# Split attention with a PReLU feed-forward layer: one mask matmul per bank ahead of the scores for batch 0's streaming heads, and a new order of the items from number 300 on

## The chip, the cores and the metric

One core of one Trainium2 chip runs the kernel. The metric is the device time of one execution in microseconds (us). Of the kernel before, three runs are known: 228.17 us in the median, 227.71 to 228.29.

## What is computed

Attention over 4 batches, 8 heads, 768 positions and 64 values per head, then a feed-forward layer on the 3072 tokens of width 512. Heads 0, 2 and 6 ("retrieval heads") are causal. The other five ("streaming heads") see only the first 4 positions (the sinks) and the last 64. The reference, cut to what matters:

```python
causal = rel >= 0
stream_keep = causal & (is_sink | in_win)          # n_sink 4, window 64
scores = where(retrieval head ? causal : stream_keep, q @ k.T / 8, -1e9)
x = softmax(scores) @ v                            # to 3072 x 512
h = x @ w_in                                       # 512 -> 2048
g = max(h, 0) + alpha * min(h, 0)
out = g @ w_out                                    # 2048 -> 512, float32
```

## The kernel before, in words

**Items and their order.** The whole kernel is a list of 1076 named items in a hand-written string, `ORDER` (L14 to L71). A loop (L807) emits them one after the other. Each engine works through its own instructions strictly in that order, and semaphores make it wait for what an instruction needs. An item's first letter says what it does:

- `L`, `C`: a load from HBM (SyncE's queue), and the cast of what was loaded to bfloat16.
- `T`/`t` (batches 0 and 1): queries or keys are transposed on TensorE and copied out. `D` (batches 2 and 3): they are transposed by a DMA from SyncE's queue (`dma_q` L321, `dma_k` L336).
- `S`, `s`, `m`: scores of a part of one head on TensorE, exp of them on ScalarE, and, from segment 4 on, the multiplication with a 0/1 mask on VectorE.
- `A`, `a`: the product with v (L553), then division by the row sum on VectorE (`AV_out`, L563 and L564).
- `X`: the head pair's result is turned into the feed-forward layer's input xT, by a DMA transpose from SyncE's queue (`X_dma`, L568) for segments 4 to 14.
- `P`, `p`, `g`: first feed-forward product (`P1`, L598), ScalarE's part of PReLU (L603), VectorE's part (L610).
- `O`, `o`: second product in quarters (`P2`, L618), copy out on ScalarE (L624) and the store, from GpSimd's queue (L628).

**Tiling.** Work comes in 16 segments, n = 0 to 15: four per batch, each a pair of heads from `PAIRS` = (2,6), (1,5), (0,4), (3,7). So `S12.0.3` is the fourth part of the scores of the first head of segment 12, the first segment of batch 3. The feed-forward layer works in 8 blocks of tokens, two per batch (512 and 256 tokens), so `P4.8` belongs to the first block of batch 2. A `P` item adds up four matmuls over the four segments of its batch, in the order of the segments. So the first `P2` item needs X4, X5, X6 and X7 one after the other, the first `P4` item X8 to X11, and the first `P6` item X12 first.

**What fixes the order around the change.** `P`, `O` and attention items of different batches are mixed in `ORDER`, so that TensorE has matmuls of the feed-forward layer to do while ScalarE and VectorE work on attention. PSUM has 8 banks of 128 x 512 float32. Which bank an item gets is settled when the kernel is built, by the order (`take`, `give`). SyncE's queue issues loads and DMA transposes in the order of the items, one after the other.

**Bursts.** Scores of segments from 4 on aren't emitted at once: `one_score` (L412) collects them, and `emit_burst` (L418) writes them out when an item comes that can't stand beside them (`beside_burst`, L435). If both heads of a pair of row halves have at least 576 columns, the matmuls use only 64 rows each, and those of the two heads run side by side on the two halves of the array (L431). Otherwise they run one after the other (L424).

**The masks of batch 0.** Segments 0 to 3 are masked by adding -30000 in PSUM: for streaming heads, each score matmul of 192, 148 or 44 columns (L414, started by `start=True`) is followed by a matmul of the identity with a mask of the same width (L502), which adds to it. `THIRD` (L482) lists the widths: seven per head, and two or three fill one bank with 384 columns. The masks `nms` and, for the last width, `nms6` are made on GpSimd (`sink_mask`, L267). Segments 1 and 3 have two streaming heads each, and segment 2 has one: five heads with 35 mask matmuls.

Of the kernel before, what the change touches and what calls it, by code (L numbers as in the profile page):

```python
# [31 lines left out]
s6.1.0 O0.3.1 a5.1 s4.0.5 O0.3.2 O0.3.3 m4.0.1 m4.0.5 Cv4 tq7 S7.0.0 S6.0.5 S7.1.1 S4.1.1 Lk9 Lk10 Lq9 o0.2 o0.3
S4.1.3 S7.0.1 A5.0 s4.1.1 s7.0.0 m4.0.0 a5.0 X5 A4.0 s7.0.1 Lk11 s7.1.1 a4.0 s4.1.3 O1.1.0 m4.1.3 Cv7 s6.0.5 m7.0.0
m7.1.1 Lq8 S7.1.0 S6.0.4 S7.0.2 S4.1.5 S6.0.1 S7.1.2 S6.1.1 O1.1.1 Cv6 s7.1.0 O1.0.0 s4.1.5 m7.0.1 s6.1.1 m4.1.5
m6.1.1 s7.1.2 m6.1.0 s7.0.2 m7.0.2 S6.0.2 S4.1.2 S6.1.2 S6.0.0 s6.0.4 s4.1.2 s6.0.1 s6.1.2 O1.0.1 m6.0.5 m7.1.0 m4.1.1
m4.1.4 m7.1.2 m6.1.2 S6.0.3 A4.1 s6.0.0 m6.0.0 m6.0.1 A7.1 O1.1.2 A6.1 s6.0.3 m6.0.4 m6.0.3 s6.0.2 a4.1 a6.1 A6.0 A7.0
a6.0 O1.1.3 O0.0.0 O0.0.1 O0.0.2 O1.0.2 m10.0.2 O1.0.3 O0.0.3 o0.0 X4 X6 a7.1 a7.0 X7 P2.9 P2.3 p2.9 P3.4 Ck9 Cq9 g2.9
P2.14 p2.14 g2.14 Cq8 p3.4 Lq10 Lq11 Dk8.0 P2.10 p2.10 Dk9.1 o1.0 p2.3 g2.3 g3.4 Dk8.1 P3.2 P3.14 P3.12 P2.8 Dq8 P2.1
P3.8 o1.1 p3.2 Dk9.0 Lv10 g2.10 Dq9 p3.14 P2.7 Ck10 g3.2 p3.12 g3.12 g3.14 P2.2 p2.2 g2.2 Cq10 Dq10 P2.11 p2.1 g2.1
p2.11 p2.8 g2.11 P3.6 P2.5 p2.5 g2.5 P2.13 p2.13 g2.8 g2.13 P2.0 p2.0 g2.0 p2.7 P3.0 p3.0 P2.4 S8.0.5 Lv8 Lv11 P2.15  # L40
P2.12 s8.0.5 Cq11 g3.0 p2.15 g2.7 g2.15 S8.0.0 p2.12 g2.12 Ck11 p3.6 S9.0.2 P2.6 p2.6 g3.6 s8.0.0 p2.4 g2.4 g2.6
s9.0.2 p3.8 P3.10 g3.8 p3.10 O3.0.0 O2.0.0 S8.1.5 s8.1.5 O3.0.1 O2.0.1 g3.10 m8.0.0 Cv8 S8.1.3 S9.0.0 S8.0.3 S9.1.1
S8.0.1 S9.1.0 s8.1.3 s9.1.0 s8.0.1 s9.0.0 s8.0.3 m8.0.3 m8.0.1 O2.0.2 O2.0.3 o2.0 Dk10.1 Lv9 m9.0.0 Cv9 m8.0.5 Dk11.0
m9.1.0 m9.0.2 S8.0.4 S9.0.1 S10.1.1 S8.1.4 Dq11 s8.1.4 Lq13 Lk13 O3.0.2 Dk10.0 s9.1.1 s10.1.1 s9.0.1 s8.0.4 O3.0.3
o3.0 Dk11.1 S10.1.0 S10.1.2 m9.0.1 S11.0.2 S9.1.2 S8.0.2 S11.0.0 s9.1.2 Cv10 m9.1.1 A9.0 s11.0.2 s10.1.0 O2.3.0 m9.1.2
A9.1 a9.0 a9.1 X9 s10.1.2 s11.0.0 O2.3.1 Lq15 Lv14 Lq12 S8.1.0 S11.0.1 S10.0.3 m10.1.0 s8.0.2 S10.0.1 S8.1.2 S8.1.1
S10.0.0 O2.3.2 s8.1.2 s8.1.0 m8.1.4 Cq13 s11.0.1 s8.1.1 m11.0.2 m10.1.2 m8.0.4 m11.0.0 A8.0 s10.0.0 m8.1.5 m10.1.1
O2.3.3 a8.0 S11.1.2 S10.0.4 S11.1.0 S10.0.5 S10.0.2 m8.1.3 m11.0.1 s10.0.3 s10.0.1 S11.1.1 s11.1.2 A10.1 s11.1.1
O2.2.0 O2.1.0 s10.0.4 m6.0.2 m10.0.1 Cv11 m8.1.1 m8.1.0 a10.1 m10.0.4 Ck13 m10.0.0 m11.1.2 A11.0 A8.1 O2.1.1 s10.0.2
s10.0.5 o2.3 s11.1.0 Dk13.0 m11.1.1 m10.0.3 m10.0.5 m11.1.0 A10.0 a11.0 a8.1 a10.0 O3.1.0 A11.1 Cq12 O2.2.1 O2.2.2  # L50
O2.2.3 a11.1 X8 O2.1.2 O3.1.1 O3.1.2 X10 o2.2 O3.1.3 O2.1.3 X11 P4.11 o2.1 P4.14 P5.14 p5.14 P4.4 P4.6 Lk12 P5.0 g5.14
Ck12 p4.4 p4.6 p4.11 P4.13 g4.6 p4.14 g4.11 Lq14 g4.14 P5.12 P4.5 P4.12 p4.13 Dq12 o3.1 p5.0 g4.13 Cq14 g5.0 Dk13.1
p4.5 g4.5 g4.4 Cv14 P4.9 p4.9 g4.9 P4.2 P5.2 Dq13 p5.12 g5.12 P4.10 p5.2 P4.8 P4.1 p4.12 g4.12 g5.2 p4.10 g4.10 Lv15
Dk12.0 Dk12.1 Lv12 p4.1 Lk14 Lv13 Lk15 g4.1 P4.7 P4.0 p4.2 g4.2 p4.8 g4.8 p4.0 p4.7 g4.7 P4.15 Cv12 S13.0.1 s13.0.1
S12.0.5 S12.0.3 P4.3 P5.4 g4.0 s12.0.3 p4.3 s12.0.5 S12.1.5 S12.0.1 S12.0.0 S13.1.1 s13.1.1 Dq14 g4.3 Cq15 Ck14
m12.0.3 O4.3.0 s12.1.5 s12.0.1 O4.3.1 O4.3.2 s12.0.0 p4.15 g4.15 P5.6 P5.10 S12.1.1 S12.0.4 S12.0.2 p5.4 S13.1.0 g5.4
p5.6 s12.0.4 Dk14.0 P5.8 s13.1.0 s12.0.2 p5.8 s12.1.1 m12.0.0 g5.6 O4.3.3 Ck15 p5.10 g5.8 m12.0.1 g5.10 m12.0.4 O5.1.0
Cv13 O5.1.1 O5.1.2 o4.3 Dk14.1 S14.1.1 S14.0.0 S12.1.4 S14.0.1 S14.1.0 S13.0.2 m12.1.1 s14.1.0 s13.0.2 O4.2.0 m12.0.5
A12.0 s14.0.1 s12.1.4 O5.1.3 Dk15.1 s14.1.1 Dk15.0 s14.0.0 a12.0 m14.0.1 Dq15 o5.1 O4.2.1 S13.1.2 S12.1.2 S14.1.2
S14.0.4 m13.1.0 m14.0.0 m13.0.1 S14.0.5 S13.0.0 O4.2.2 O4.2.3 s13.1.2 m13.1.2 m13.1.1 s13.0.0 s14.0.4 s14.0.5 m13.0.2  # L60
S12.1.0 m12.1.5 s14.1.2 S12.1.3 S15.0.0 S14.0.3 m13.0.0 A13.1 o4.2 s12.1.0 s12.1.2 A13.0 s15.0.0 O5.0.0 s12.1.3
s14.0.3 m14.0.4 Cv15 a13.1 O5.0.1 a13.0 S15.0.1 S15.0.2 m12.1.0 S15.1.0 S15.1.2 S15.1.1 S14.0.2 O4.1.0 s15.0.2 s15.1.0
m12.1.4 s14.0.2 s15.1.1 m14.1.1 m14.0.5 m14.1.2 m12.1.3 m14.1.0 A12.1 m14.0.3 A14.1 A14.0 a14.0 s15.1.2 a14.1 m15.0.2
s15.0.1 a12.1 O4.1.1 X13 O4.0.0 O4.0.1 O4.0.2 O4.0.3 m15.0.0 m15.1.1 O4.1.2 m15.0.1 m15.1.2 m15.1.0 A15.0 o4.0 A15.1
a15.0 O4.1.3 a15.1 O5.0.2 X15 O5.0.3 X14 x15 o4.1 o5.0 X12 P6.11 p6.11 P6.2 P6.15 P6.10 p6.10 P7.4 P6.0 P6.1 g6.11
g6.10 p6.1 P6.6 P7.8 p6.15 g6.15 g6.1 p6.0 g6.0 P6.5 p7.4 p6.5 p6.6 g7.4 g6.6 g6.5 P6.3 P6.12 P7.2 p6.3 p6.12 g6.12
# [8 lines left out]
def kernel(  # L75
# [336 lines left out]
    def one_score(n, hh, m, to, keys, queries, stop=True):  # L412
        if n < 4:
            nc.tensor.matmul(to, keys, queries, start=True, stop=stop)  # L414
# [69 lines left out]
    def thirds(n, m):  # L484
        return (range(0, 2), range(2, 3))[m] if n < 4 else range(m, m + 1)

    def S_stream(n, hh, m):
# [8 lines left out]
        for x, part in enumerate(thirds(n, m)):
            o = 0
            for j, w in THIRD[part]:
                one_score(n, hh, m, sc[:, x, o:o + w], kt[:, 128 * j:128 * (j + 1)],
                          qt[:, 124 * j:124 * j + w], n >= 4)  # L500
                if n < 4:
                    nc.tensor.matmul(sc[:, x, o:o + w], ident, (nms6 if j == 6 else nms)[:, 0:w],  # L502
                                     start=False, stop=True)
# [344 lines left out]
```

## Time and profile before

| what | value |
|---|---|
| median of 3 runs | 228.17 us (227.71 to 228.29) |
| the profiled execution's own time | 228.43 us |
| its span in the profile | 225.8 us, so 2.6 us lie around it |
| TensorE (PE) busy | 221.6 us, 2005 matmuls |
| VectorE (DVE), ScalarE (ACT), GpSimd (POOL) busy | 149.1, 140.1, 45.9 us |
| granted TensorE clock | 1.00 from 5.7 us on |
| moved by DMA | 37.39 MB, mean 166 GB/s |

How to read it: the span runs from the first to the last instruction of one profiled execution. Times in the text that stand alone ("at 80.72") are microseconds from the span's start. A matmul's own duration overlaps with the next one's, so its cost to TensorE is the distance from one start to the next. A DMA has an issue (an instruction in the issuing engine's queue) and a landing (the last of its semaphore events in the trace).

### The profile page before, as it was taken

Reading aid. Unit: us, or ns where it says so; the run is one execution under the profiler, and the core shown is the slowest. Engines: PE = TensorE matmul, PEld = TensorE weight load, DVE = VectorE, ACT = ScalarE, POOL = GpSimd, SP = SyncE. Lnnn points to the kernel's source line nnn. Section 1 sums busy time; section 2 is a strip of 40 time slices with the busy share of each in tenths; the row PEclk is TensorE's granted clock in tenths of the full one; section 3 lists DMA queues with packets and bytes.
Section 4 is the critical chain, followed back from the end, with each engine's and each line's share of the span. In section 5 each row is a group of like instructions: output and inputs, shape, how many; then the busy total and the mean of one; then the engine's idle time right before and its main releaser. Section 6 shows DMA issues by size and latency. Waiting matters only on the chain.

```text
span 225.8 us, 5241 instructions
## 1 busy us (share of the span) xinstructions
PE 221.6 (98%) x2005; PEld 136.5 (60%) x2005; DVE 149.1 (66%) x393; ACT 140.1 (62%) x286; POOL 45.9 (20%) x91
## 2 busy tenths in 40 slices
...
PEclk9999999999999999999999999999999999999999
DMA  6999999999999999999989999976924420000213
GB/s 201 311 240 214 281 223 285 197 196 231 204 284 182 117 232 231 170 167 190 268 160 177 226 243 129 238 156 117 119 94 38 120 93 0 0 3 1 93 68 119
DMA packets 95417, 37.39 MB, mean 166 GB/s; under 512 B 82440, under 2 KB 93600, under 8 KB 95392
## 3 DMA queue, kind: packets, MB, share of 16 engines
...
q8 instruction: 15, 0.25, 0.5%
...
## 4 chain that ended last, share of the span: by engine, by line
PE 98%; DVE 0%; issue 0%; DVEq 0%
PE P L598 37%; PE P L618 36%; PE P L553 7%; PE P L431 4%; PE P L414 3%; PE P L688 3%; PE P L364 2%; PE P L637 2%; PE P L424 1%; PE P L502 1%; PE P L578 1%; PE P L463 0%; PE P L362 0%; DVE kT L387 0%; DVE ot L646 0%
## 5 line engine op out<-in xcount | busy, mean ns | idle before, releaser
L610 DVE SCALAR_TENSOR_TENSOR g<-neg,oma,P 128x256 bf16<-128x256 f32 (+1 forms) x128 | 70.9, 608 | 36.9 <-ACT neg L603 36.4
L598 PE MATMUL P<-xT,w_in_b 128*128 128x512 bf16 (+1 forms) x512 | 86.6, 326 | 0.0
L618 PE MATMUL P<-w_out_b,g 128*128 128x512 bf16 x368 | 85.3, 379 | 0.0
L603 ACT ACTIVATE neg<-P 128x512 f32<-128x512 f32 x96 | 54.2, 600 | 26.3 <-PE P L598 20.9
L598 PEld LDWEIGHTS <-w_in_b 128*128 128x128 bf16 x512 | 49.5, 98 | 32.3 <-DVE g L610 0.2
L618 PEld LDWEIGHTS <-g 128*128 128x128 bf16 x368 | 33.9, 98 | 37.2 <-issue 1.0
L470 ACT ACTIVATE eR<-P 128x448 bf16<-128x448 f32 (+4 forms) x63 | 36.9, 635 | 5.8 <-PE P L431 2.5
L624 ACT COPY ot<-P 128x512 f32<-128x512 f32 x23 | 13.9, 605 | 37.1 <-PE P L618 32.3
L628 POOL DMA_DIRECT2D out_dram<-ot x18 | 10.3, 572 | 111.0 <-ACT ot L624 110.8
L518 ACT ACTIVATE eS<-P 128x352 bf16<-128x352 f32 x45 | 20.8, 489 | 3.4 <-PE P L431 3.0
L564 DVE TENSOR_TENSOR xn<-P,rcp 128x448 bf16<-128x448 f32 (+1 forms) x32 | 19.5, 608 | 1.1
L529 DVE TENSOR_TENSOR eS<-eS,ms_near 128x352 bf16<-128x352 bf16 x45 | 14.9, 346 | 0.6 <-ACT eS L518 0.5
L563 DVE RECIPROCAL rcp<-P 128x7 f32<-128x7 f32 (+1 forms) x32 | 6.3, 198 | 10.9 <-PE P L553 10.8
L480 DVE TENSOR_TENSOR eR<-eR,mr_near 128x128 bf16<-128x128 bf16 (+5 forms) x54 | 10.7, 227 | 4.3 <-ACT eR L470 4.1
L414 PE MATMUL P<-qT,kT 128*128 128x192 bf16 (+14 forms) x68 | 11.2, 251 | 0.2 <-DVE kT L387 0.2
L553 PEld LDWEIGHTS <-eS 128*128 128x128 bf16 x260 | 9.5, 97 | 2.3 <-issue 0.6
L553 PE MATMUL P<-vb,eS 128*128 128x65 bf16 x260 | 10.7, 193 | 0.0
L431 PE MATMUL P<-qT,kT 64*128 64x176 bf16 (+10 forms) x168 | 10.5, 252 | 0.0
L431 PEld LDWEIGHTS <-kT 64*128 64x128 bf16 x168 | 6.7, 94 | 6.2 <-issue 5.5
L553 PE MATMUL P<-vb,eR 128*128 128x65 bf16 x276 | 10.5, 193 | 0.0
L553 PEld LDWEIGHTS <-eR 128*128 128x128 bf16 x276 | 9.5, 97 | 1.3
L646 DVE COPY ot<-P 128x128 f32<-128x128 f32 x1 | 0.3, 291 | 14.3 <-PE P L637 14.3
...
## 6 DMA issues: line engine op xcount, KB each, us to landing
...
```

What stands on the lines that cost most here:

```text
L414: nc.tensor.matmul(to, keys, queries, start=True, stop=stop)
L431: nc.tensor.matmul(to, keys[own], queries[own], start=True, stop=True)
L470: nc.scalar.activation(ebuf[n, hh][:, lo:hi].rearrange("p (x c) -> p x c", x=len(parts)), P[:, got[0]:got[0] + len(parts), 0:(hi - lo) // ...
L518: nc.scalar.activation(slots, sc[:, 0:352].rearrange("p (s c) -> p s c", c=176), AF.Exp, scale=scale)
L529: nc.vector.tensor_tensor(slots, slots, ms_near[:, 0:2, :] if m == 0 else ms_near[:, 1:3, :], op=ALU.mult)
L553: nc.tensor.matmul(pav[:, i, :], e[:, o:o + 128], vv[:, j, hh, 0:D + 1], start=(m == 0), stop=(m == len(terms) - 1))
L564: nc.vector.tensor_tensor(xn[n][:, 0:nt, D * hh:D * hh + D], pav[:, :, 0:D], rcp.to_broadcast([128, nt, D]), op=ALU.mult)
L598: nc.tensor.matmul(psg[:, w * i:w * (i + 1)], w_in_b[:, c, 128 * fb:128 * (fb + 1)], xT[:, c, o:o + w], start=(x == 0), stop=(x == 3))
L603: nc.scalar.activation(neg[t, f], bank(held["P", t, f][0]), AF.Relu, scale=-1.0)
L610: nc.vector.scalar_tensor_tensor(g_buf[t % 2][:, fb, 0:w], neg[t, f][:, c], oma[:, fb:fb + 1], bank(got[0])[:, c], op0=ALU.mult, op1=ALU.add)
L618: nc.tensor.matmul(bank(held["O", t, s][0]), g_buf[t % 2][:, f, 128 * s:128 * (s + 1)], w_out_b[:, f, :], start=(f == 0), stop=(f == 15))
L624: nc.scalar.copy(ot, bank(got[0]))
```

## The change

There are two parts.

**Masks.** For each bank of a streaming head in batch 0, one matmul of the identity with a mask of 384 columns comes first and starts the bank. The scores of this bank then add to it, with no mask behind each. The last third (192, 148 and 44 columns) has a mask of its own, the second row of a new tile `nms2`. GpSimd makes it with one copy more.

```diff
-    nms = const.tile([128, 192], bf16, name="nms")
-    nms6 = const.tile([128, 44], bf16, name="nms6")
+    nms2 = const.tile([128, 2, 192], bf16, name="nms")
+    nms = nms2[:, 0, :]
...
-        nc.gpsimd.tensor_copy(nms6, nms[:, 0:44])
-        nc.gpsimd.memset(nms6[0:NSINK, 0:NSINK], OUT)
+        nc.gpsimd.tensor_copy(nms2[:, 1, 0:148], nms[:, 0:148])
+        nc.gpsimd.tensor_copy(nms2[:, 1, 148:192], nms[:, 0:44])
+        nc.gpsimd.memset(nms2[0:NSINK, 1, 148:148 + NSINK], OUT)
...
         for x, part in enumerate(thirds(n, m)):
+            nc.tensor.matmul(sc[:, x, 0:384].rearrange("p (a c) -> p a c", c=192), ident,
+                             nms2 if part == 2 else nms2[:, 0:1, :].to_broadcast([128, 2, 192]),
+                             start=True, stop=False)
+        for x, part in enumerate(thirds(n, m)):
             o = 0
             for j, w in THIRD[part]:
-                one_score(n, hh, m, sc[:, x, o:o + w], kt[:, 128 * j:128 * (j + 1)],
-                          qt[:, 124 * j:124 * j + w], n >= 4)
-                if n < 4:
-                    nc.tensor.matmul(sc[:, x, o:o + w], ident, (nms6 if j == 6 else nms)[:, 0:w],
-                                     start=False, stop=True)
+                nc.tensor.matmul(sc[:, x, o:o + w], kt[:, 128 * j:128 * (j + 1)], qt[:, 124 * j:124 * j + w],
+                                 start=False, stop=o + w == 384)
                 o += w
```

**Order.** The same 1076 items are kept. Items 0 to 299 stay where they are; from number 300 (about 48 us into the span) to number 1019 they stand in a new order. SyncE's queue keeps its order: all its 154 loads, transposes and stores are issued in the same sequence. What moves are the matmuls, the exps, the casts and the copies around them. Three stretches, first before and then after. The end of batch 1's attention:

```
before: ... A6.1 s6.0.3 m6.0.4 m6.0.3 s6.0.2 a4.1 a6.1 A6.0 A7.0 a6.0 O1.1.3 O0.0.0 O0.0.1 O0.0.2 O1.0.2 m10.0.2 O1.0.3
        O0.0.3 o0.0 X4 X6 a7.1 a7.0 X7 P2.9 P2.3 p2.9 P3.4 Ck9 Cq9 ...
after:  ... A7.0 m6.0.0 m6.1.1 A6.1 m6.0.3 a7.1 Ck9 m6.0.5 a4.1 a6.1 s6.0.2 X4 A6.0 a6.0 X6 Ck8 a7.0 X7 Lq10 O0.0.1 Cq8
        O1.0.1 O0.0.2 O0.0.3 o0.0 O1.0.2 O1.0.3 P2.14 ...
```

The end of batch 2's attention and the way to batch 3's first scores:

```
before: A10.0 a11.0 a8.1 a10.0 O3.1.0 A11.1 Cq12 O2.2.1 O2.2.2 O2.2.3 a11.1 X8 O2.1.2 O3.1.1 O3.1.2 X10 o2.2 O3.1.3 O2.1.3
        X11 P4.11 o2.1 ... 18 more P items, o3.1 and SyncE's items as below ... S13.0.1 s13.0.1 S12.0.5 S12.0.3
after:  A10.0 a8.1 O2.2.2 O2.2.3 o2.2 m11.1.2 Lv14 Lq12 Dk13.0 a10.0 A11.1 a10.1 O2.1.0 O2.1.1 X8 a11.1 X10 X11 Lk12
        O2.1.2 O2.1.3 P4.8 P4.6 P4.11 P4.14 P4.10 P5.2 P4.5 P4.1 Lq14 Dq12 Dk13.1 Dq13 P5.12 Lv15 P4.4 P5.14 O3.1.3
        Dk12.0 Dk12.1 Lv12 P5.6 o2.1 o3.1 P4.13 P4.0 S12.0.3     (p, g and C items between them are left out)
```

The end of batch 3's attention:

```
before: A12.1 m14.0.3 A14.1 A14.0 a14.0 s15.1.2 a14.1 m15.0.2 s15.0.1 a12.1 O4.1.1 X13 O4.0.0 O4.0.1 O4.0.2 O4.0.3 ...
        A15.0 o4.0 A15.1 a15.0 O4.1.3 a15.1 O5.0.2 X15 O5.0.3 X14 x15 o4.1 o5.0 X12 P6.11
after:  A12.1 O5.0.3 a14.0 O4.0.2 a14.1 O4.1.2 X14 a12.1 O4.1.3 a15.0 a15.1 X15 O4.0.3 x15 X12 P6.4
```

More of the change, by code (lines that the diff above doesn't have):

```diff
@@ L32 @@
[L32 to L66, printed above, removed]
@@ new lines @@
+s4.0.4 m4.0.4 s6.1.0 O0.2.3 o0.2 A5.1 O0.3.2 O0.3.3 a5.1 Cv4 o0.3 S4.1.1 S7.0.1 S4.1.3 S6.0.5 S7.1.1 S7.0.0 s4.1.3
+s7.1.1 m4.1.4 ro1 m4.0.0 A5.0 a5.0 A4.0 s4.1.1 O1.1.0 s6.0.5 S6.0.4 S7.1.0 S6.1.1 a4.0 m4.1.0 s7.0.0 S7.0.2 S6.0.1
+s7.0.1 m7.0.1 S4.1.5 s7.1.0 m7.1.0 s6.0.4 m6.1.0 Lq9 X5 O1.1.1 O1.1.2 S6.0.3 S6.0.2 s6.0.1 m6.0.1 S4.1.2 Lk11 s4.1.5
+S7.1.2 m6.0.4 m4.1.5 S6.1.2 m4.1.1 s6.1.1 S6.0.0 m4.1.3 Lq8 O1.1.3 near1 s7.0.2 O0.0.0 s7.1.2 Cv6 m7.1.1 m7.1.2 A7.1
+s6.1.2 m6.1.2 m10.0.2 s6.0.3 m7.0.0 s6.0.0 O1.0.0 s4.1.2 A4.1 m7.0.2 A7.0 m6.0.0 m6.1.1 A6.1 m6.0.3 a7.1 Ck9 m6.0.5
@@ new lines @@
+a4.1 a6.1 s6.0.2 X4 A6.0 a6.0 X6 Ck8 a7.0 X7 Lq10 O0.0.1 Cq8 O1.0.1 O0.0.2 O0.0.3 o0.0 O1.0.2 O1.0.3 P2.14 P3.12 P2.9
+p2.9 P2.6 p2.14 Lq11 g2.14 g2.9 p3.12 g3.12 P2.7 P2.10 p2.10 g2.10 P2.1 p2.1 g2.1 Dk8.0 P2.2 Dk9.1 Dk8.1 Cq9 p2.2 g2.2
+p2.7 g2.7 p2.6 P2.3 P2.13 p2.13 g2.6 Ck10 Dq8 Cq10 P2.5 P2.11 Dk9.0 p2.5 P2.4 o1.0 o1.1 g2.5 g2.13 p2.11 g2.11 S8.0.0
+s8.0.0 Lv10 Ck11 P3.4 Dq9 Dq10 Lv8 p2.4 g2.4 Lv11 P2.8 p2.8 P3.2 Cq11 p2.3 p3.2 g3.2 g2.3 P3.0 g2.8 p3.0 g3.0 P2.0
+p2.0 g2.0 S8.1.5 s8.1.5 P3.6 P3.14 p3.14 g3.14 P2.15 p3.6 g3.6 p2.15 g2.15 S9.0.2 s9.0.2 S8.0.5 P2.12 P3.10 P3.8 p3.4
@@ new lines @@
+g3.4 p3.8 Dk10.1 Lv9 O3.0.0 O3.0.1 p2.12 g2.12 O2.0.0 O2.0.1 p3.10 s8.0.5 S9.0.0 g3.8 S8.0.1 S8.0.3 S9.1.1 g3.10
+m6.0.2 S8.1.3 S9.1.0 s9.1.1 m9.1.1 s9.1.0 s8.1.3 O2.0.2 O2.0.3 s8.0.3 S10.1.1 S9.0.1 s9.0.0 S8.1.4 s8.0.1 S8.0.4
+s8.0.4 m9.1.0 m8.1.5 Cv10 s9.0.1 s10.1.1 m9.0.2 m8.0.1 Dk11.0 Cv8 Dq11 O3.0.2 m8.0.0 O3.0.3 S11.0.2 S11.0.0 s8.1.4
+S8.0.2 S10.1.2 S9.1.2 o2.0 Lq13 Lk13 S10.1.0 Cv9 O2.3.0 m9.0.0 s9.1.2 s10.1.0 m9.0.1 m8.0.4 m10.1.1 m9.1.2 Dk10.0
+Dk11.1 o3.0 A9.0 s11.0.0 A9.1 m8.1.4 m8.0.5 O2.3.1 m8.0.3 s8.0.2 A8.0 a9.0 a9.1 s10.1.2 S8.1.1 s11.0.2 S10.0.3 S11.0.1
@@ new lines @@
+m11.0.2 S8.1.2 S8.1.0 S10.0.0 s10.0.0 m10.0.0 s8.1.0 a8.0 O2.3.2 O2.3.3 m8.1.0 O3.1.0 s11.0.1 s8.1.1 S10.0.4 m8.1.1
+m11.0.1 S11.1.0 s10.0.3 o2.3 S11.1.2 S11.1.1 s8.1.2 S10.0.5 S10.0.1 O3.1.1 s10.0.5 Cq13 Cv11 s11.1.1 S10.0.2 m11.0.0
+s10.0.4 s10.0.1 A11.0 O3.1.2 m8.1.3 A8.1 m10.0.4 m10.1.0 s10.0.2 a11.0 s11.1.0 m10.1.2 m11.1.0 A10.1 m10.0.3 O2.2.0
+O2.2.1 Ck13 s11.1.2 m10.0.1 X9 Lq15 m10.0.5 m11.1.1 A10.0 a8.1 O2.2.2 O2.2.3 o2.2 m11.1.2 Lv14 Lq12 Dk13.0 a10.0 A11.1
+a10.1 O2.1.0 O2.1.1 X8 a11.1 X10 X11 Lk12 O2.1.2 O2.1.3 P4.8 p4.8 Cq12 P4.6 p4.6 g4.8 P4.11 P4.14 P4.10 p4.10 P5.2
@@ new lines @@
+p4.14 g4.6 g4.14 Ck12 P4.5 p4.5 g4.5 P4.1 Lq14 Dq12 Dk13.1 p4.1 g4.10 Dq13 P5.12 Lv15 P4.4 Cv14 p5.2 g5.2 p4.4 g4.4
+P5.14 O3.1.3 p5.12 g4.1 Dk12.0 Dk12.1 Lv12 P5.6 g5.12 p4.11 Cq14 p5.14 g4.11 o2.1 p5.6 o3.1 g5.6 g5.14 P4.13 p4.13
+g4.13 P4.0 p4.0 S12.0.3 s12.0.3 S13.0.1 P4.12 p4.12 g4.12 s13.0.1 Lk14 Lv13 P4.2 p4.2 P5.0 g4.0 p5.0 g4.2 g5.0 m12.0.3
+S12.0.5 s12.0.5 Cv12 P4.3 p4.3 S13.1.1 Lk15 S12.0.0 S12.1.5 S12.0.1 s12.0.1 m12.0.1 s12.1.5 P5.4 p5.4 g4.3 s13.1.1
+m13.1.1 P4.9 p4.9 s12.0.0 P4.7 Ck14 p4.7 g5.4 P5.8 p5.8 g4.7 g5.8 Cq15 Dq14 Dk14.0 Dk14.1 P5.10 m12.1.5 P4.15 S12.1.1
```

20 lines of the change are left out of this document (15 added, 5 removed).

## The prediction, made before the changed kernel ran

> **What bounds the kernel now.** I read the page first. TensorE (PE) is busy for 98% of the span, at full clock, and the chain that ended last is PE for 98%:
>
> ```profile
> PE 221.6 (98%) x2005; PEld 136.5 (60%) x2005; DVE 149.1 (66%) x393; ACT 140.1 (62%) x286; POOL 45.9 (20%) x91
> ...
> PEclk9999999999999999999999999999999999999999
> DMA  6999999999999999999989999976924420000213
> ...
> PE 98%; DVE 0%; issue 0%; DVEq 0%
> ```
>
> The reader should see two things: an engine without gaps, and DMA engines that are nearly as full until about 165 us. But "busy" hides waits, because a matmul's row lasts longer than its distance to the next. So I read the timeline of PE for distances between starts:
>
> ```profile
> 20.54 0.24 PE L414 MATMUL P<-qT,kT 128*128 128x192 bf16 x1
> 20.62 0.24 PE L502 MATMUL P<-nms,ident 128*128 128x192 bf16 x1
> 20.70 0.25 PE L414 MATMUL P<-qT,kT 128*128 128x192 bf16 x1
> ...
> 21.49 0.18 PE L414 MATMUL P<-qT,kT 128*128 128x44 bf16 x1
> 21.52 0.18 PE L502 MATMUL P<-nms,ident 128*128 128x44 bf16 x1
> ```
>
> Each 192-column matmul costs 0.082 us (a row of 0.24 us), a 44-column one 0.028. In the same way 512 columns cost 0.216, 384 cost 0.163, 256 cost 0.109, and 65 cost 0.029. Starts further apart than these distances are rare: 0.78 us of waits before 26 us, 0.14 at 52.9, and around each of the 15 split bursts (L431) about 0.10 ahead and 0.13 within and behind. Else nothing. So the time is PE's sum of distances, plus each wait that a new order creates; no later slack pays a wait back. That is why I weigh the change by waits.
>
> **Masks.** Removed: 25 x 0.082 + 5 x 0.064 + 5 x 0.028 = 2.51 us. Added: 15 of 384 columns x 0.163 = 2.45 us (no row shows a mask of this form; rows of 384 columns elsewhere range from 0.161 to 0.164, so 2.42 to 2.46). Gain 0.06. All of it falls before 26 us, where PE also waits for VectorE's and ScalarE's copies, so part becomes waiting: 0 to 0.06. GpSimd's extra copy (0.22 us by the 44-column row) falls into its idle 0.85 us ahead of the cast at 4.69: nothing.
>
> **Bursts.** Walking through both orders with L435's rule gives 15 split bursts in each. Taking for each the larger half of its matmuls' distances, the sum goes from 7.99 to 7.93 us; the unsplit ones go from 3.03 to 3.05. Gain 0.04. Together PE's sum falls by 0.1 us.
>
> **The waits that the order creates.** SyncE's sequence is unchanged, so what matters is which producer now comes later and which consumer earlier. In before, the nearest escape was the first P2 item: X7 landed at 80.29 and its matmul ran at 80.72. X11 had 2.9 us to spare, X12 3.0, Dk12.0 (needed by S12.0.3) 4.7. I laid the same places out in the new order.
>
> First P2 item. VectorE's rows (timeline, 73 to 77 us):
>
> ```profile
> 73.84 0.21 DVE L563 RECIPROCAL rcp<-P 128x7 f32<-128x7 f32 x1
> 74.08 0.62 DVE L564 TENSOR_TENSOR xn<-P,rcp 128x448 bf16<-128x448 f32 x1
> 74.62 0.20 DVE L563 RECIPROCAL rcp<-P 128x7 f32<-128x7 f32 x1
> 74.85 0.63 DVE L564 TENSOR_TENSOR xn<-P,rcp 128x448 bf16<-128x448 f32 x1
> 75.39 0.20 DVE L563 RECIPROCAL rcp<-P 128x7 f32<-128x7 f32 x1
> 75.62 0.62 DVE L564 TENSOR_TENSOR xn<-P,rcp 128x448 bf16<-128x448 f32 x1
> 76.16 0.62 DVE L334 CAST natk<-kf 128x896 bf16<-128x896 f32 x1
> ```
>
> They are a6.0, a7.1, a7.0, then Ck9. In the new order a7.1 (0.78) and Ck9 (0.53) stand ahead of a6.0, and Ck9 and Ck8 (1.06) ahead of a7.0. So a6.0 ends at 74.70 + 1.3 = 76.0 and a7.0 at 76.24 + 1.1 = 77.3; the masks moved about may add 0.2. X7 can't issue before 77.35 and, at the landing time of 2.80 that X7 had, lands at 80.15 to 80.35; its matmul is at 80.72 - 0.1 = 80.6. No wait, by 0.3. But X6's issue took 2.66 us in before (the queue's instruction held up), against 1.25 for most transposes. If X6 again holds the queue that long from 76.05, X7 issues at 78.8, lands at 81.6, and PE waits 1.0. Bounds 0 to 1.2; I take 0.2, near the common row.
>
> First P4 item and S12.0.3. X10 waits for a10.1, and a10.1 now stands behind a10.0 on VectorE. From the start of A10.0's last matmul: 0.19 us to its end, 0.03 to a10.0, 1.70 for a10.0 and a10.1 (rows at 122.45 and 123.69: 0.86 to the end of each, 0.84 from one to the next), 0.03 to the issue: X10 issues 1.95 us after. X11 follows 1.34 later and lands 2.81 after that: 6.1. PE until the first P4 item's fourth matmul: A11.1 0.38, six O items of four matmuls 5.18, three matmuls 0.65: 6.2. So X11 is just in time (bounds 0 to 0.3; I take 0).
>
> Then the SyncE queue, from X8, X10, X11 at 122.56 on:
>
> ```profile
> 122.56 3.92 SPq L572 DMA_TRANSPOSE xT<-xn  x3
> 126.54 1.16 SPq L246 DMA_DIRECT2D kf<-in_k_dram  x2
> 127.74 1.39 SPq L212 DMA_DIRECT2D qf<-in_q_dram  x2
> 129.23 1.75 SPq L322 DMA_TRANSPOSE qT<-natq  x1
> 131.03 1.30 SPq L338 DMA_TRANSPOSE kT<-natk  x1
> 132.38 2.03 SPq L322 DMA_TRANSPOSE qT<-natq  x1
> ...
> 136.92 3.70 SPq L338 DMA_TRANSPOSE kT<-natk  x2
> ```
>
> There is no gap: each issue follows the one ahead, and none waits for a producer. So Dk12.0 comes a fixed stretch after X10: issued at 136.92 - 123.90 = 13.0 after, landed (142.19) 18.3 after. In the new order S12.0.3 is the consumer, with this PE work between A10.0's last matmul and it: A11.1 0.38, six O items 5.18, fourteen P items and O3.1.3, 15 x 0.865 = 12.98: 18.5 us. Dk12.0 lands 1.95 + 18.3 = 20.2 after the same point. **PE waits 1.7 us.** What stands behind S12.0.3 on PE is everything, and nothing can pass. The lower bound is 0: with transposes at 1.3, loads at the shortest distances in that stretch (11.4 us) and the shortest landing of a transpose in the trace (2.75), Dk12.0 lands 16.1 after A10.0's point.
>
> What could shorten it? The DMA view for 124 to 142 us:
>
> ```profile
> q1 hardware_dynamic: 11026, 2.73, 89.1%
> q0 software_dynamic: 305, 0.99, 16.4%
> ```
>
> Engines are full, and the stores (q0) take 16.4%, three of them in 18 us. In the new order o2.1 and o3.1 stand behind P5.6, just ahead of S12.0.3, so two of the three leave this stretch: 2/3 x 16.4% x 18 = 1.97 us of work, as much as the wait. If the engines' load sets the pace, Dk12.0 is in time. But the same chain reaches Dk14.1, 31.4 us after X10 (123.90 to 155.33), needed by the burst that begins at S14.1.0. By the sum of PE's distances that burst starts 32.5 us after A10.0's point, Dk14.1 lands at 33.4: 0.9 us late, and by then both stores are back. So 0 to 1.7 in all for these two places (they are one delay, not two); I take 0.9.
>
> The Trainium skill ("DMA: Bandwidth & Descriptors", "Queues, rings and completion order") states that each DMA engine goes round between the queues for which it has work, packet by packet. By that rule the stores that leave would speed up SyncE's transfers at once and the sum would be about 0.9 us less; the trace shows both queues served at a time, but not by what rule.
>
> First P6 item. X12 is issued about 1.0 us after A12.1's end if VectorE is free, lands 2.8 later; PE has four O items, X15's transposes and O5.0.3 ahead, 4.7 us: 0.8 to spare. No wait.
>
> Elsewhere, banks and exps: the nearest row is the 0.14 at 52.9 (a wait for a copy of keys), which can go or come again. Bounds -0.14 to +0.3; I take 0.1.
>
> **Sum**, in the profiled execution: 225.8 - 0.1 + 0.2 + 0.9 + 0.1 = 226.9 us of span, plus the 2.6 around it, 229.5 against its 228.43. That execution is 0.26 above the median of 228.17, so I forecast 228.17 + 1.1 = **229.3 us**.
>
> **Rivals.**
>
> *Everything lands in time* (not slower). The mechanism is the stores that leave the stretch, with X6 no longer held because X4 finds the loads ahead of it already landed. For it: X8, X10 and X11 issue at 1.34 us each. It decides if X10 to Dk12.0 takes less than 16.6 us and X10 to Dk14.1 less than 30.6 instead of 18.3 and 31.4. Then only PE's sum counts: 228.17 - 0.1 = 228.1. Chance 0.28.
>
> *Both delays in full.* X6 holds the queue (1.0 to 1.2) and the chain stays as measured (1.7), with 0.1 to 0.3 elsewhere: +2.8, 231.0. Against it: part of the first delay also moves what follows. Chance 0.20.
>
> *Faster.* Masks that need no keys run while PE would wait, so the exps of the streaming heads start earlier and the 0.78 us of waits before 26 us go: 228.17 - 0.1 - 0.78 = 227.3. Against it: the longest (0.33 at 12.3) ends with a copy of keys on VectorE, which is busy without a gap from 9.0 to 13.2, and no streaming head's scores start late in the trace. Chance 0.07.
>
> That the masks don't do what they say would move nothing: they are worth 0.06.
>
> **How the numbers follow.** Forecast 0.45 (+0.7 to +2.0), rivals 0.28, 0.20 and 0.07. The range reaches from the in-time case to the full delays: 228.0 to 231.0. About 0.3% (0.7 us) is what a measurement can tell from no change. Slower by more than that: nearly all of the forecast and the second rival, 0.64; within: 0.29; faster: 0.07.
>
> **What would show it.** In the changed kernel, PE should have gaps in starts ahead of S12.0.3's scores (L425) at about 142 us, or ahead of the burst at about 156 us, and perhaps in the first P2 item (L600, third or fourth matmul) at 80 to 82 us, each ended by a DMA's landing. 15 masks at 0.163 apart would confirm the first part. If PE has no such gaps and the time is near 228.1, the chain from X10 was shorter than measured before. A time under 227.5 would say that the early waits were PE's to remove.

## The result and the profile after

The changed kernel takes **230.26 us** in the median of six runs (229.55 to 230.90), against 227.94 us for the kernel before, measured in turn with it on the same chip. The ratio is 1.0102, with a 95% interval of 1.0079 to 1.0125: slower by 2.3 us, where 1.1 was forecast. In all ratios of this text, executions that took over 1.5% longer than the fastest of their kernel are left out (one or two in six of the kernels, among them two of 591 us), while the medians are over all executions.

The profiled execution has a span of 228.9 us and took 230.58 us itself. These lines of its page answer to those shown of before:

```profile
PE 220.3 (96%) x1958; PEld 134.8 (59%) x1985; DVE 149.4 (65%) x393; ACT 140.5 (61%) x286; POOL 46.2 (20%) x92
...
PEclk9999999999999999999999999999999999999999
DMA  6999999999998899999979799984913321000213
...
PE 64%; DMA 10%; issue 7%; DVE 7%; SPq 6%; ACT 4%; POOL 1%; DVEq 0%; POOLq 0%; ACTq 0%
```

TensorE has 1985 matmuls now (the weight loads are complete, 27 records of matmuls are missing). The clock is full throughout. What changed is the last line: the chain that ended last was TensorE for 98%, and now leaves it for DMAs, VectorE and queues. TensorE waits. The view of TensorE's waits says for what (us in total, times, longest):

```profile
PE P L600 <- DVE g L612: 1.2, 2, 1.0
...
PE P L600 <- DMA xT<-xn: 1.2, 2, 0.8
```

L600 is the first feed-forward product (L598 in before; the lines behind the edit are one or two higher). The idle time in this view begins where the last matmul ended, so it is smaller than what the time loses. The loss is the distance between starts, less the 0.216 us of a 512-column matmul (0.109 for 256 columns, 0.029 for 65). The timeline of TensorE shows the places (start, duration, then in brackets the idle time and what ended it):

```profile
64.57 0.79 PE L555 MATMUL P<-vb,eR 128*128 128x65 bf16 x21
...
81.04 2.33 PE L600 MATMUL P<-xT,w_in_b 128*128 128x512 bf16 x14 [0.36 <-DMA xT<-xn]
...
98.34 1.91 PE L600 MATMUL P<-xT,w_in_b 128*128 128x256 bf16 x12 [0.95 <-DVE g L612]
...
101.09 1.13 PE L600 MATMUL P<-xT,w_in_b 128*128 128x512 bf16 x5 [0.29 <-DVE g L612]
...
133.15 2.10 PE L600 MATMUL P<-xT,w_in_b 128*128 128x512 bf16 x9 [0.83 <-DMA xT<-xn]
```

By distances between starts, TensorE lost 0.28 us ahead of 64.57 (A4.0), 0.52 ahead of 81.04 (P2.14's fourth matmul, for X7), 1.12 ahead of 98.34 (P3.6), 0.16 at 100.2 and 0.45 ahead of 101.09 (both for banks), and 0.99 ahead of 133.15 (P4.8's fourth matmul, for X11). That is 3.52 us; before had one such wait behind 26 us, of 0.14. At S12.0.3 (145.5 us) and at the burst of S14.1.0 (159.4 us), where the prediction put the main wait, there is none.

### The profile page after: what moved, and what is told of

It is laid out like the page before. It is cut to its first block, busy times and chain, and to the rows that moved or that the text cites. A ratio compares the mean times of both kernels' runs of the same rounds, so it can differ in the third digit from the quotient of the medians.

```text
span 228.9 us, 5178 instructions
## 1 busy us (share of the span) xinstructions
PE 220.3 (96%) x1958; PEld 134.8 (59%) x1985; DVE 149.4 (65%) x393; ACT 140.5 (61%) x286; POOL 46.2 (20%) x92
## 4 chain that ended last, share of the span: by engine, by line
PE 64%; DMA 10%; issue 7%; DVE 7%; SPq 6%; ACT 4%; POOL 1%; DVEq 0%; POOLq 0%; ACTq 0%
PE P L620 23%; PE P L600 23%; PE P L555 6%; SPq L242 4%; DMA xT<-xn 3%; PE P L432 3%; DMA vf<-in_v_dram 3%; DMA qT<-natq 2%; DMA qf<-in_q_dram 2%; DVE g L612 2%; PE P L639 2%; PE P L365 1%; ACT eR L471 1%; PE P L415 1%; ACT neg L605 1%
## 5 line engine op out<-in xcount | busy, mean ns | idle before, releaser
L600 PE MATMUL P<-xT,w_in_b 128*128 128x256 bf16 (+1 forms) x501 | 86.4, 325 | 3.0 <-DVE g L612 1.2
L620 PE MATMUL P<-w_out_b,g 128*128 128x512 bf16 x352 | 83.6, 379 | 0.9 <-issue 0.2
L605 ACT ACTIVATE neg<-P 128x512 f32<-128x512 f32 x96 | 55.0, 601 | 32.5 <-PE P L600 23.4
L600 PEld LDWEIGHTS <-w_in_b 128*128 128x128 bf16 x512 | 49.4, 98 | 34.6 <-issue 2.3
L630 POOL DMA_DIRECT2D out_dram<-ot x18 | 9.8, 547 | 119.6 <-ACT ot L626 119.6
L690 PE MATMUL P<-busy 128*128 128x128 bf16 x73 | 6.7, 259 | 1.2 <-DVE busy L289 1.2
```

What stands on the lines that cost most here:

```text
L600: nc.tensor.matmul(psg[:, w * i:w * (i + 1)], w_in_b[:, c, 128 * fb:128 * (fb + 1)], xT[:, c, o:o + w], start=(x == 0), stop=(x == 3))
L605: nc.scalar.activation(neg[t, f], bank(held["P", t, f][0]), AF.Relu, scale=-1.0)
L620: nc.tensor.matmul(bank(held["O", t, s][0]), g_buf[t % 2][:, f, 128 * s:128 * (s + 1)], w_out_b[:, f, :], start=(f == 0), stop=(f == 15))
```

## The experiments

Twelve kernels ran, each in turn with the kernel before on the same chip. The chips differ (e1 to e4 on one, e5 to e8, e9 to e11 and e12 on others), so kernels are compared by their ratios. The theory, after the result: masks and bursts do nothing, and each wait above has one late producer behind it. The rival: the stretches are full, and a wait that is taken away comes back at the next item.

| run | kernel | median, us | ratio to before (95%) |
|---|---|---|---|
| e1 | new masks, before's order | 227.96 | 0.9994 (0.9981 to 1.0006) |
| e2 | old masks, new order | 230.60 | 1.0102 (1.0079 to 1.0124) |
| | after | 230.26 | 1.0102 (1.0079 to 1.0125) |
| e3 | after, Cq11 later | 229.19 | 1.0043 (1.0025 to 1.0060) |
| e4 | after, stores o1.0 and o1.1 earlier | 229.42 | 1.0078 (1.0052 to 1.0104) |
| e5 | after, Ck9 and Ck8 behind X7 | 230.16 | 1.0089 (1.0059 to 1.0119) |
| e6 | after, O3.1.3 ahead of P4.8 | 230.69 | 1.0125 (1.0089 to 1.0162) |
| e7 | after, Cv4 ahead of o0.2 | 229.68 | 1.0061 (1.0029 to 1.0092) |
| e8 | e3, e5, e6 and e7 together | 229.81 | 1.0095 (1.0060 to 1.0129) |
| e9 | e6, two stores back in X10's stretch | 231.52 | 1.0132 (1.0072 to 1.0192) |
| e10 | e5, O1.0.0 behind X7 | 230.26 | 1.0071 (1.0034 to 1.0107) |
| e11 | e8, O1.0.0 behind X7, Cq14 later | 228.71 | 1.0017 (0.9990 to 1.0043) |
| e12 | e11, s4.1.2 earlier, Cv14 later | 229.25 | 1.0055 (1.0029 to 1.0081) |

The edits are moves of items in `ORDER`; the diffs show only the items around them.

### Which part costs: e1 and e2

e1 has the new masks and before's order; e2 the old masks and the new order.

> The new masks with the order of before. Theory 'late transfers' (the whole slowdown comes from the new order: TensorE waits for X7 in the first P2 item, 0.5 us, for a PSUM bank while VectorE stands in Cq11 behind Dq9, 1.7 us, and for X11 in the first P4 item, 1.0 us): no change that can be measured, 0 to -0.2 us against before, masks 0.163 us apart. Rival 'masks' (a mask that starts a whole bank ahead of the scores costs time, in itself or by making exps wait longer): +0.5 us or more.

> The new order with the masks of before. 'Late transfers': as slow as the changed kernel, +2.2 to +2.5 us against before, with the same three waits on TensorE (0.5 at 80, 1.7 between 97 and 101, 1.0 at 132). 'Masks': nearer to before, +1.5 us or less.

e1 is level with before and e2 with after, both within 0.25%. **The order costs everything, the masks nothing.** (e1 has times, but no profile that can be compared.) In e2's profile the waits are shared out otherwise than in after's: 1.49 us at P2.14's fourth matmul, 0.46 at P4.8's, none at 97 us. So they are no fixed sum: the same order gives other waits in another execution.

### The wait at 97 us: e3 and e4

VectorE's timeline in after, at that place:

```profile
93.89 0.74 DVE L612 SCALAR_TENSOR_TENSOR g<-neg,oma,P 128x512 bf16<-128x512 f32 x1
96.94 0.56 DVE L316 CAST natq<-qf 128x768 bf16<-128x768 f32 x1 [2.31 <-issue]
```

The cast is Cq11. VectorE stands still for 2.31 us in front of it, and the g items behind it, which free TensorE's banks, stand still with it. The page names no releaser ("issue"), but the code does: `NATQ` has two buffers (L181), so Cq11 overwrites the queries that the DMA transpose Dq9 reads. Dq9 was issued at 91.38 and landed at 96.86; Cq11 starts 0.08 us later. In before Dq9 landed 3.23 us after its issue, not 5.48, and Cq11 stood 2.8 us behind that. The stores o1.0 and o1.1 are issued at 91.46 and 91.99 in after; in before they were at 86.1 and 87.1, ahead of Dq9. Cq11 in before, without a wait:

```profile
97.46 0.55 DVE L315 CAST natq<-qf 128x768 bf16<-128x768 f32 x1
```

```diff
-P2.8 p2.8 P3.2 Cq11 p2.3 p3.2 g3.2 g2.3 P3.0 g2.8 p3.0 g3.0 P2.0 p2.0 g2.0 S8.1.5
+P2.8 p2.8 P3.2 p2.3 p3.2 g3.2 g2.3 P3.0 g2.8 p3.0 g3.0 P2.0 p2.0 g2.0 Cq11 S8.1.5
```

> The changed kernel with one item moved: Cq11 stands behind g2.0, some 4 us of TensorE work later. 'Late transfers': VectorE no longer idles 2.3 us behind Dq9, the waits between 97 and 101 go, -1.0 to -1.7 us against the changed kernel (+0.6 to +1.3 against before); the waits for X7 and X11 stay. Rival 'banks' (TensorE at 97 waits because of the order of the P items and their banks, whatever VectorE does): no change, +2.3 against before.

e3 is 0.6% faster than after, as expected. Its Dq9 was as late (5.32 us), but Cq11 now comes behind the g items and waits for nothing, and TensorE has no wait between 95 and 102 us:

```profile
99.91 0.55 DVE L316 CAST natq<-qf 128x768 bf16<-128x768 f32 x1
```

e4 leaves Cq11 where it is and issues the two stores at 88.1 us, some 3 us earlier:

```diff
-P2.1 p2.1 g2.1 Dk8.0 P2.2 ... Dk9.0 p2.5 P2.4 o1.0 o1.1 g2.5
+P2.1 p2.1 g2.1 o1.0 o1.1 Dk8.0 P2.2 ... Dk9.0 p2.5 P2.4 g2.5
```

> The changed kernel with the stores o1.0 and o1.1 moved ahead, from behind P2.4 (issued at 91.2 and 91.7) to behind g2.1 (about 85 us). If Dq9's landing (5.5 us after its issue, in before 3.2) is late because these two stores share the DMA engines with it: Dq9 lands 1.5 to 2.5 us earlier, VectorE's idle time in front of Cq11 shrinks from 2.3 to under 0.8, and the time falls by 0.8 to 1.7 us against the changed kernel. If the stores have no part in it (the loads Lv10 ahead of Dq9 in its own queue hold it): no change, +2.3 against before.

By the ratios it gained about 0.5 us, less than expected, and the intervals overlap. Dq9 landed after 3.23 us, as the theory said, but Cq11 still had to wait for it, for 0.51 us:

```profile
95.58 0.56 DVE L316 CAST natq<-qf 128x768 bf16<-128x768 f32 x1 [0.51 <-DVE g L612]
```

It starts 0.08 us behind Dq9's landing (95.50) again, and TensorE still loses 0.29 at 100 us. So the place of Cq11 is shown as the cause of the loss. What makes Dq9 late goes with the time of the stores, and not with their place in `ORDER`. GpSimd's timelines in after and in e5, where Dq9 is issued at 91.38 and 92.67:

```profile
91.46 1.07 POOL L630 DMA_DIRECT2D out_dram<-ot  x2 [11.70 <-ACT ot L626]
...
93.38 1.08 POOL L630 DMA_DIRECT2D out_dram<-ot  x2 [12.61 <-ACT ot L626]
```

| first of the two stores | profiles | Dq9 lands after, us |
|---|---|---|
| 0.04 to 0.19 us behind Dq9's issue | after, e3, e6, e7, e8, e9, e11 | 5.2 to 6.1 |
| 0.63 to 0.87 us behind it | e2, e5, e12 | 3.1 to 3.6 |
| over 4 us ahead of it | before, e4 | 3.2 |

Only e4 moved the stores by intent, so this is a pattern of twelve profiles; what happens in the DMA engines no run shows.

### GpSimd's queue: e7

The 0.28 us at A4.0 came in each of the profiles with Cv4 in its new place. GpSimd's timeline in after:

```profile
63.02 0.56 POOL L630 DMA_DIRECT2D out_dram<-ot  x1 [2.28 <-ACT ot L626]
63.57 0.94 POOL L350 CAST vb<-vf 128x896 bf16<-128x896 f32 x1
```

The cast is Cv4, which makes A4.0's values. Its load had landed at 62.50, but it stands behind o0.2's store, and that waits for ScalarE's copy. The cast ends at 64.51, A4.0 starts at 64.57. In before Cv4 stood ahead of o0.2 and started at 62.76, when its load had landed:

```profile
62.76 0.93 POOL L349 CAST vb<-vf 128x896 bf16<-128x896 f32 x1 [1.55 <-DMA vf<-in_v_dram]
```

```diff
-O0.2.3 o0.2 A5.1 O0.3.2 O0.3.3 a5.1 Cv4 o0.3
+O0.2.3 Cv4 o0.2 A5.1 O0.3.2 O0.3.3 a5.1 o0.3
```

> The kernel after with the cast of values Cv4 moved ahead of the store of o0.2 on GpSimd, where the kernel before has it. Theory (a queue that the order moved it behind): in after the cast starts at 63.57, behind the issue of a store that waits for its eviction, and ends at 64.51, when A4.0 starts 0.28 us late; ahead of the store it starts when its load has landed (62.5) and ends about 63.4, the wait of 0.28 us at A4.0 is gone, and the time falls by 0.1 to 0.3 us, to 229.9 to 230.1. Rival: the 0.28 us is the price of the change of weights or is taken up by the waits behind it: 230.2, and the gap ahead of A4.0 stays.

The gap at A4.0 is gone, here and in e8, e11 and e12. (e7's profiled execution took 234.89 us, for a wait at 29 us that the last section shows; e8's shows the same without it.) The time fell by 0.9 us against after by the ratios, with intervals that just overlap; 0.28 of it is explained by this gap.

### The transfers X7 and X11: e5, e6 and e10

> The kernel after with two casts of keys (Ck9, Ck8) moved behind X7 on VectorE. Theory (late transfers): the casts stand ahead of a6.0 and a7.0, so both end about 0.6 us earlier, X7 is issued and lands about 0.6 us earlier, and the wait at the fourth matmul of P2.14 (0.52 us in the profile of after, 1.49 with the order alone) shrinks by about 0.6 us; the other waits stay, and they may take up some of it: 0.2 to 0.7 us less than after, about 229.6 to 230.1. Rival: X7 is held by the queue behind X6's own issue, not by a7.0, and the wait and the time stay as they are.

```diff
-a7.1 Ck9 m6.0.5 a4.1 a6.1 s6.0.2 X4 A6.0 a6.0 X6 Ck8 a7.0 X7 Lq10
+a7.1 m6.0.5 a4.1 a6.1 s6.0.2 X4 A6.0 a6.0 X6 a7.0 X7 Ck9 Ck8 Lq10
```

The rival was right: the time is after's, and the wait in this profile is larger, 1.43 us. SyncE's and TensorE's timelines:

```profile
75.12 5.89 SPq L574 DMA_TRANSPOSE xT<-xn  x3
...
82.96 2.33 PE L600 MATMUL P<-xT,w_in_b 128*128 128x512 bf16 x14 [1.27 <-DMA xT<-xn]
```

The three issues of X4, X6 and X7 take 5.89 us, because X6's takes 2.82. a7.0 ended at 77.56, but X7 was issued at 79.79. This is the held queue that the prediction had as a bound. Over eight profiles:

| | before | after | e2 | e3 | e5 | e6 | e8 | e12 |
|---|---|---|---|---|---|---|---|---|
| X6's issue takes, us | 2.66 | 1.85 | 1.34 | 1.29 | 2.82 | 1.78 | 2.01 | 1.21 |
| X4's issue to X7's landing, us | 7.47 | 6.56 | 7.52 | 5.95 | 7.80 | 6.53 | 6.72 | 5.87 |
| first P2 item waits, us | 0 | 0.52 | 1.49 | 0 | 1.43 | 0.49 | 0.35 | 0 |

In all but e2, X6's issue ended 0.5 to 1.2 us before X4 landed. In e2, which has the longest wait, it was X4's own issue that was held: it took 2.17 us, and 1.2 in the others. In the new order P2.14 starts 5.4 to 5.8 us after X4's issue, and its first three matmuls cover 0.6 more; in before the first P2 item, P2.9, starts 7.3 us after it. So the wait is the length of this train less a cover of 6.0 to 6.4 (in e5, 7.80 - 5.76 - 0.6 = 1.44), and the train differs from profile to profile of kernels that are nearly alike up to there. What holds an issue is not shown.

e10 was to bring X4 forward, with e5's move and this one:

```diff
-m7.0.0 s6.0.0 O1.0.0 s4.1.2 A4.1 m7.0.2 A7.0
+m7.0.0 s6.0.0 s4.1.2 A4.1 m7.0.2 A7.0
...
-a7.0 X7 Ck9 Ck8 Lq10 O0.0.1 Cq8 O1.0.1
+a7.0 X7 Ck9 Ck8 Lq10 O0.0.1 Cq8 O1.0.0 O1.0.1
```

> The kernel of e5_x7_early with one matmul group of the output projection (O1.0.0, 0.86 us) moved from ahead of A4.1 to behind X7, so that A4.1, a4.1 and X4 come up to 0.86 us earlier while the first P2 item stays where it is. Theory (X4 sets the pace: in every profile X6's issue ends 0.5 to 1.2 us before X4 lands, and X7 is issued only behind it): X4 and X7 land 0.5 to 0.9 us earlier against the start of P2.14, its wait falls from 1.43 (e5) or 0.52 (after) to between 0 and 0.6, and the time is 0.3 to 0.9 us under that of e5, 229.3 to 229.9. Rival: X4 lands when the loads ahead of it on the queue have, not earlier; X7 and the wait stay, 230.2.

Inconclusive: 1.0071 lies between e5's 1.0089 and the gain expected, and there is no profile that can be compared. e11 and e12, which contain the same move, show that less comes of it than the 0.86 us hoped for: X4 is issued 6.2 and 5.6 us ahead of P2.14 there, and 5.8 in e8. VectorE does a7.1 ahead of a4.1, which may be why.

e6 covers X11 instead of bringing it forward:

```diff
-O2.1.2 O2.1.3 P4.8 p4.8 Cq12 ... P5.14 O3.1.3 p5.12
+O2.1.2 O2.1.3 O3.1.3 P4.8 p4.8 Cq12 ... P5.14 p5.12
```

> The kernel after with one matmul group of the output projection (O3.1.3, four matmuls, 0.86 us) moved from among the P5 items to right ahead of P4.8. Theory (late transfers): it covers X11's landing, so the wait at the fourth matmul of P4.8 (0.99 us in the profile of after, 0.46 to 0.72 in three others) falls to 0.0 to 0.15 and the time by 0.4 to 0.9 us, to 229.4 to 229.9. Rival: X11 is only one of several late things there, and the next P4 or P5 items wait in its place: no change, 230.2.

P4.8's wait is gone, and the time did not fall. Part of it came back 9 to 12 us later, 0.14 in P5.14 and 0.42 ahead of S13.0.1, both for a bank. That is the rival, and e8 shows the engine behind it; the waits of this profile do not explain the whole of the time.

### All of them, and the new bound: e8, e11 and e12

> The kernel after with all four moves: Ck9 and Ck8 behind X7, Cv4 ahead of o0.2's store, Cq11 behind g2.0, and O3.1.3 ahead of P4.8. Theory (the new order lost only by these four waits, some 2.9 us in the profile of after): all four are gone, and the time is 227.2 to 228.0, level with the kernel before or up to 0.3% under it. Rival: the waits move on to the next late transfer, and the time stays above 228.8.

e8 failed its expectation: 229.81. In its profile the waits at A4.0, 97 us and P4.8 are gone, 0.35 is left at P2.14, and 0.14 and 0.42 stand where e6 has them. VectorE's timeline, and TensorE's at S13.0.1:

```profile
139.59 2.97 DVE L612 SCALAR_TENSOR_TENSOR g<-neg,oma,P 128x256 bf16<-128x256 f32 x6
142.47 0.55 DVE L316 CAST natq<-qf 128x768 bf16<-128x768 f32 x1
142.94 2.31 DVE L612 SCALAR_TENSOR_TENSOR g<-neg,oma,P 128x512 bf16<-128x512 f32 x5
...
143.74 0.31 PE L425 MATMUL P<-qT,kT 128*128 128x176 bf16 x2 [0.26 <-DMA vf<-in_v_dram]
```

The bracket is not the releaser here: that load has nothing to do with scores. S13.0.1 needs a bank that g4.11 frees, the first g at 142.94; it ends at 143.68, and S13.0.1 starts 0.05 later. VectorE has no gap from 136.5 us on, and the cast at 142.47 is Cq14, which is needed by Dq14 alone, some 9 us later. So **VectorE is the bound of this stretch** once X11 no longer slows TensorE: 0.66 us from one g to the next (142.94 to 143.60) against 0.86 for a P item, and three casts besides. It had stood idle for 2.33 us just before, with no g to do until ScalarE's part of the item was done.

e11 moves Cq14 out of the way, and O1.0.0 as in e10:

```diff
-p4.11 Cq14 p5.14 g4.11 o2.1 p5.6 o3.1 g5.6 g5.14 P4.13 p4.13 g4.13 P4.0
+p4.11 p5.14 g4.11 o2.1 p5.6 o3.1 g5.6 g5.14 P4.13 p4.13 g4.13 Cq14 P4.0
```

> The kernel of e8_all_four with two more moves: O1.0.0 behind X7 as in e10, and the cast Cq14 moved on VectorE from ahead of g4.11 to behind g4.13 (in e8 and e6 the matmul of S13.0.1 starts 0.42 us late, right after g4.11 ends and frees its bank; VectorE worked without a gap before it). Theory (each wait has one late producer): the 0.42 at S13.0.1 and the 0.35 at P2.14 are gone, and the time is 0.5 to 1.2 us under that of e8, 228.6 to 229.3. Rival (the waits move on to the next item because VectorE and the queues are full there): the time stays at 229.8.

The theory held: 228.71, 0.8% under e8, and at most 0.43% above before by the interval, which includes 1. Its profile has no wait over 0.1 us at P2.14, at P4.8 or at S13.0.1. But Cq14 has its price in the new place too: it stands at 150.20, and TensorE loses 0.47 us at 152.78 for a bank that a g behind it frees (e3 and e4 lose less than 0.1 there). And the profiled execution of e11 took 233.29 us: some 4 us of it were lost at this wait and in the slow clock behind it (see the last section), ahead of every item that moved:

```profile
32.02 0.51 PE L365 MATMUL P<-ident,natm 128*128 128x128 bf16 x6 [2.25 <-POOL natm L329]
```

With these six moves nearly all of the loss is back, and what the masks and the rest of the order cost can't be told from nothing.

e12 tried for the rest, moving Cv14 from ahead of p5.2 to behind g4.1 on VectorE, and s4.1.2 ahead of s6.0.0:

```diff
-P4.4 Cv14 p5.2 g5.2 p4.4 g4.4 P5.14 p5.12 g4.1 Dk12.0
+P4.4 p5.2 g5.2 p4.4 g4.4 P5.14 p5.12 g4.1 Cv14 Dk12.0
...
-s6.0.3 m7.0.0 s6.0.0 s4.1.2 A4.1
+s6.0.3 m7.0.0 s4.1.2 s6.0.0 A4.1
```

> The kernel of e11_six with two small moves more: the exp s4.1.2 ahead of s6.0.0 on ScalarE (in e11's profile A4.1 has a gap of 0.20 us) and the cast Cv14 behind g4.1 on VectorE (a gap of 0.15 us in P5.14, behind g4.10). Theory (the new order costs its waits and nothing else; PE's sum of distances is that of before less 0.1): without them it is level with before, 227.7 to 228.5, a ratio between 0.998 and 1.002. Rival (something in the new order that the profiles of waits do not show costs 0.5 us or more): 228.7 to 229.5.

It failed. The cast now stands at 141.67, just ahead of the g items that S13.0.1 waits for, and about half of e11's gain over e8 is gone (the intervals of e11 and e12 overlap): 0.23 us lost ahead of S12.0.3 and 0.37 at S13.0.1. It fits the bound of this stretch, by a miss. No kernel of the study beats before.

### The stores in X10's stretch: e9

```diff
-P4.11 P4.14 P4.10 ... P5.12 Lv15 ... Cq14 p5.14 g4.11 o2.1 p5.6 o3.1 g5.6
+P4.11 o2.1 P4.14 P4.10 ... P5.12 o3.1 Lv15 ... Cq14 p5.14 g4.11 p5.6 g5.6
```

> The kernel of e6_p4_cover with the evictions and stores of o2.1 and o3.1 moved back into the stretch between X10 and Dk12.0 (behind P4.11 and behind P5.12; after and e6 have both behind P5.6). In the profile of e6 Dk12.0 lands 15.0 us behind X10's issue, in after 16.2, in before, where both stores lie in the stretch, 18.3. Theory (the stores' work holds up SyncE's transfers, some 2 us for the two): Dk12.0 lands 16.5 to 17.5 us behind X10, and S12.0.3 begins to wait for it: 0 to 0.8 us more than e6 in time. Rival: the stretch was shorter in the new order for another reason (VectorE's casts earlier, fewer loads held up), Dk12.0 lands 15.0 to 15.5 us behind X10, and the time stays as in e6.

Dk12.0 landed 19.3 us behind X10's issue (e6 15.0, after 16.2, before 18.3). The issue itself was only 0.9 us later than in e6, at 12.8; the landing took 6.4 us instead of 3.1. In this profile S12.0.3 waits for it, and the waits of TensorE and the windows around it (busy, granted clock, DMA share, GB/s) read:

```profile
PE P L425 <- DMA kT<-natk: 2.4, 1, 2.4
...
142.00:147.00 5.00, 2.62 (x17) 1.00 1.15 133
147.00:150.60 3.60, 3.54 (x12) 0.55 1.35 225
```

So the stores' place decides whether Dk12.0 is in time, as the theory said, by more than it said: in the ten profiles with o2.1 and o3.1 behind the stretch it landed 15.0 to 16.4 us behind X10's issue, in the two with both in it (before and e9) 18.3 and 19.3. In e9 the store of o3.1 was issued 0.22 us behind Dk12.0, the same closeness as with Dq9 above. In e9's other three executions the span was 1.7 to 2.9 us shorter, so this wait is not always so long, and against e6 the time is not clearly different.

## Why the prediction was right or wrong

- **What bounds the kernel: right.** The time is TensorE's sum of distances plus its waits. With most of the waits removed (e11) it can't be told from before's time, and is at most 0.43% above it.
- **Masks: right.** 15 masks cost 0.162 us each, 2.43 in all, and e1 measures no difference. The 0.04 us of the bursts is less than any run could show.
- **First P2 item: mechanism right, mis-sized.** a6.0 ended at 75.94 and a7.0 at 77.25, as worked out (76.0 and 77.3). X7 landed at 80.99 instead of 80.15 to 80.35, because X6's issue took 1.85 us. I took 0.2 of 0 to 1.2; the profiles have 0 to 1.49, and after's 0.52. The working treated a7.0 as the likely limit; e5 shows that it is the queue, which in e2 was held at X4 and not at X6.
- **First P4 item: wrong by one term.** X10 was issued 1.99 us after the start of A10.0's last matmul (1.95 predicted) and X11 1.33 later (1.34). But X11 landed 3.88 us after its issue, not the 2.81 that it had in before. I called it "just in time" and took one landing time from before's profile, with an upper bound of 0.3; the loss was 0.99. This was no chance of one execution: X11 took 3.4 to 3.9 us to land in all eleven profiles with the new order, where the store of o2.2 is issued 0.4 to 0.5 us ahead of it (in before 1.9 behind it). No run moved that store, so its part is not shown.
- **S12.0.3 and S14.1.0: the largest term, and it was nothing.** I took 0.9 of 0 to 1.7; it is 0. Dk12.0 landed 16.2 us behind X10's issue instead of 18.3, and Dk14.1 30.5 instead of 31.4, 1.1 us ahead of its burst, so the rival's mechanism (stores that leave the stretch) was the right one here. The DMA view of after for 124 to 142 us:

```profile
q1 hardware_dynamic: 11022, 2.73, 90.4%
q0 software_dynamic: 80, 0.26, 4.9%
```

  The stores' share fell from 16.4% to 4.9%, and the chain became 2.1 us shorter, against the 1.97 worked out; e9 puts the stores back and gets 19.3. By the rule of the Trainium skill that was named ("DMA: Bandwidth & Descriptors", "Queues, rings and completion order"), engines that go round between queues packet by packet, this is what should happen. These profiles agree with it, though none shows by what rule the queues are served.
- **First P6 item: right.** X12 landed at 183.07, 0.9 us ahead of P6.4 (0.8 predicted).
- **"Elsewhere" (0.1, at most 0.3): the step that failed most.** It cost 2.01 us in after's profile: 1.73 at 97 to 101 us and 0.28 at A4.0. I had looked only for transfers that TensorE waits for. Both losses come from another engine's queue: VectorE behind Cq11, which waits until a transpose has *read* a buffer, and GpSimd's Cv4 behind a store that waits. That SyncE's sequence is unchanged did not protect them, since casts and stores moved against it.
- **The sum.** 229.3 was forecast and 230.26 came: 1.2 us of waits foreseen, 3.5 in the profile. That the kernel is slower, and by waits, was rightly seen; that the time lies in the range is in good part luck. The largest foreseen term (0.9) did not come, and 3.0 us came at places for which 0.1 was put down. "Both delays in full" (231.0) comes nearer in time, but not for its reason: one of its delays was 0.5, the other nothing.

Two things stay open. The gains of the single moves don't add up to e11's (e3 alone is below e8, which contains it, with intervals that just touch). And e8's profiled execution had a span of 227.0 us, the five others that are alike 227.8 to 228.4: some of what the typical execution loses is in no profile.
